# Keys turned by VectorE in 32x32 blocks, and first-softmax scores as 32-row by 32-column array tiles in three banks

## The chip, the cores and the metric

The kernel runs on one core of a Trainium2 chip. The metric is the device time in microseconds of one execution. Three runs of the kernel before took 1696.77, 1696.78 and 1698.92 us; their median is 1696.78 us.

## What is computed

Three stages follow each other, all in fp32: an attention with 32 learned "pack" rows per head, a gated feed-forward layer, and a second feed-forward layer.

```python
# q, k, v: (8 batches, 8 heads, 576, 64); p: (8, 8, 32, 64)
def sm_attn(qq, kk, vv):
    s = scale * np.matmul(qq, kk.transpose(0, 1, 3, 2))
    s = s - np.max(s, axis=-1, keepdims=True)
    a = np.exp(s)
    a = a / (np.sum(a, axis=-1, keepdims=True) + 1e-09)
    return np.matmul(a, vv)
p_packed = sm_attn(p, k, v)                # first softmax: 32 x 576 scores per head
out = sm_attn(q, p_packed, p_packed)       # second softmax: 576 x 32 scores per head
...
x = out as (4608 tokens, 512); xn = x / rms(x) * rms_g
x = (silu(xn @ w_gate) * (xn @ w_val)) @ w_out          # 512 -> 1536 -> 512
h = x @ w_in2; return (max(h,0) + alpha*min(h,0)) @ w_out2   # 512 -> 2048 -> 512
```

The change is in the first softmax alone, up to its exponentials: `p @ k^T`, the row maximum, and exp. The weights and `w_in2`, `w_out2` arrive as 64-bit numbers and are narrowed on the chip.

## The kernel before, in words

**Main loop.** Tokens are worked in 12 chunks `c` (`CH`, L49 to L60) of 512 or 320 columns, three for each two batches. In each chunk a loop over `f` from 0 to 11 (L951) does a gate block `ps_g` (`blk_in`, L967), a value block `ps_v` (L978), and, for the `f` before, the block back to the model width `ps_y` (`blk_out`, L985). Each product is three matmuls of split operands (`mm3`, L121 to L123). VectorE combines gate and value at L975 and L979, ScalarE takes the high part `hh` and VectorE the low part `hl`.

**Work between the blocks.** The attention of later batches is cut into steps of generators ("chains"): `k_steps` for the first softmax of one batch, `q_steps` for the second softmax of a group of tokens. `burst(f)` (L922) emits their TensorE work between the value block and `blk_out`, within a budget of 4 PSUM banks; a weight job `wg_job` takes 2 of them. A step that yields a number waits for a burst with that many left. `work(f, at)` (L875) emits the other steps: `E` (any engine) one per call, `R` (reads of a bank), and `M` and `X` (maximum and exp). In chunks after the first, `M` and `X` come in the call right behind the burst. In chunks 0 and 1 the key chain goes first in a burst, later the query chains do.

**Banks.** Gate, value, weight-job and attention blocks take turns in four PSUM banks (tag `m`, L105), in program order: each new block waits until the last reader of the block four places earlier is done.

**One key chain** (a batch; 8 heads in two groups `g` of 4). `load_p` and `load_kv` bring p and the keys with heads side by side. S1 (L358) and S2 (L367) turn p and the keys with TensorE transposes, 4 and 24 per batch; `evac` copies each bank to SBUF on ScalarE (L116) or VectorE (L118). S3 (L377) makes the scores of two heads at a time with p laid out block-diagonally, so half of the 128 contracted rows meet zeros: 4 matmuls of 288 columns for each group, in two banks. fp32 matmuls appear in the trace as two passes each. MX (L387, L388) takes the maximum on VectorE, EX (L397) the exponentials on ScalarE, RZ (L403, L407) the reciprocal of the sum. S4 (L415) turns the exponentials, S5 (L424) multiplies by v, S6 (L446) prepares the second softmax.

**Prologue.** Before the main loop, the chain of batch 0 and the query chains of the first 512 tokens run alone (L688 to L748), beside the first weight loads. All loads are issued by SP, in program order.

Of the kernel before, what the change touches and what calls it, by code (L numbers as in the profile page):

```python
# [8 lines left out]
F32 = mybir.dt.float32  # L9
# [9 lines left out]
def attention_moe_moe2_kernel(ctx, tc, q, k, v, p, w_gate, w_val, w_out, rms_g, w_in2, w_out2, alpha, out):  # L19
# [105 lines left out]
    with tc.manual_schedule():  # L125
# [6 lines left out]
        pbd = ap.tile([64, H // 2, 128], F32, name="pbd")  # L132
        ppbd = [ap.tile([128, G, HG, D], F32, name=f"ppbd{i}") for i in range(2)]
        ppB = [ap.tile([128, HG, NP], F32, name=f"ppB{i}") for i in range(2)]
        nc.vector.memset(pbd, 0.0)
# [8 lines left out]
        def load_p(b):  # L144
            for e in range(2):
                for g in range(G):
                    nc.sync.dma_start(
                        out=pbd[(e ^ g) * NP:(e ^ g) * NP + NP, 2 * g:2 * g + 2, e * D:(e + 1) * D],
                        in_=p[b].rearrange("(g c e) n d -> e g n c d", g=G, e=2)[e, g],
                    )  # L150
# [4 lines left out]
        def load_kv():  # L155
# [5 lines left out]
            if nm == "k":  # L161
                t = t.rearrange("p (r h) d -> p r h d", r=KR)
                for h in range(HG):
                    nc.sync.dma_start(out=t[:, :, h], in_=src[:, h])
            else:
                t = t.rearrange("p (h r) d -> p h r d", r=KR)
                nc.sync.dma_start(out=t, in_=src)
# [180 lines left out]
        def k_steps(b, bk):  # L348
            par = b % 2
            yield 2  # L350
            pT = ap.tile([128, H // 2, 64], F32, tag="pT", name="pT")
            s1, kT, E1, E1T = {}, {}, {}, {}
            st = [ap.tile([128, 8], F32, tag=f"st{g}", name=f"st{g}") for g in range(G)]

            def S1():
                t = bk()
                for c in range(4):
                    nc.tensor.transpose(t[:, c * 64:(c + 1) * 64], pbd[:, c, :], ident[0:64, 0:64])  # L358
                return lambda: evac(pT, t[:, 0:256].rearrange("p (c x) -> p c x", c=4), True)

            def S2(g, n):
                t = bk()
                if n == 0:
                    kT[g] = ap.tile([128, 2 * S], F32, tag="kT", name="kT")
                for m in range(4):
                    c, r = divmod(4 * n + m, KR)
                    nc.tensor.transpose(  # L367
                        t[:, m * KP:(m + 1) * KP], kv_t[b, "k", g][:, r, 2 * c:2 * c + 2, :], ident[0:KP, 0:KP]
                    )
                return lambda: evac(kT[g][:, n * 384:(n + 1) * 384], t[:, 0:384], n % 2 == 0 or b < 2)  # L370

            def S3(g):
                w = S // 2
                for hf in range(2):
                    t = bk()
                    for c in range(2):
                        nc.tensor.matmul(  # L377
                            out=t[c * 64:(c + 1) * 64, 0:w],
                            lhsT=pT[:, 2 * g + c, :],
                            rhs=kT[g][:, c * S + hf * w:c * S + (hf + 1) * w],  # L380
                            start=True, stop=True,
                        )
                    s1[g, hf] = t

            def MX(g):
                for hf in range(2):
                    nc.vector.tensor_reduce(out=st[g][:, hf:hf + 1], in_=s1[g, hf][:, 0:S // 2], axis=AX.X, op=ALU.max)  # L387
                nc.vector.tensor_scalar(  # L388
                    out=st[g][:, 2:3], in0=st[g][:, 0:1], scalar1=st[g][:, 1:2], scalar2=-scale,
                    op0=ALU.max, op1=ALU.mult,  # L390
                )

            def EX(g):
                w = S // 2
                E1[g] = ap.tile([128, S], F32, tag="E1", name="E1")
                for hf in range(2):
# [87 lines left out]
            if b + 1 < B:  # L484
                load_p(b + 1)
# [237 lines left out]
        for n in range(9):  # L723
            ck.run()
            if n == 7:
                qa.run()
# [505 lines left out]
```

## Time and profile before

| | |
|---|---|
| median of three runs | 1696.78 us |
| the profiled execution | 1693.4 us, span 1691.6 us, mean granted clock 0.98 |
| TensorE matmul busy | 1610.1 us, 95% of the span |
| VectorE, ScalarE, GpSimd busy | 1129.2 us (67%), 708.5 us (42%), 356.0 us (21%) |
| chain that ended last | TensorE 74%, VectorE 13%, ScalarE 4% |
| DMA queue | 52.3% of 16 engines' span |

The profile comes from one execution, 1.8 us of it outside the span. Busy time of TensorE counts the tail of each pipelined matmul, so it overstates the work a little; where one block ends and the next begins is read from the timeline or the chain. The key chains of batches 1 to 7 lie between 46 and about 677 us of the span.

### The profile page before, as it was taken

Reading aid. Unit: us, or ns where it says so; the run is one execution under the profiler, and the core shown is the slowest. Engines: PE = TensorE matmul, PEld = TensorE weight load, DVE = VectorE, ACT = ScalarE, POOL = GpSimd, SP = SyncE. Lnnn points to the kernel's source line nnn. Section 1 sums busy time; section 2 is a strip of 40 time slices with the busy share of each in tenths; the row PEclk is TensorE's granted clock in tenths of the full one; section 3 lists DMA queues with packets and bytes.
Section 4 is the critical chain, followed back from the end, with each engine's and each line's share of the span. In section 5 each row is a group of like instructions: output and inputs, shape, how many; then the busy total and the mean of one; then the engine's idle time right before and its main releaser. Section 6 shows DMA issues by size and latency. Waiting matters only on the chain.

```text
span 1691.6 us, 28163 instructions
## 1 busy us (share of the span) xinstructions
PE 1610.1 (95%) x10378; PEld 1353.6 (80%) x10378; DVE 1129.2 (67%) x2109; ACT 708.5 (42%) x1529; POOL 356.0 (21%) x321
## 2 busy tenths in 40 slices
PE   7787998999999899999998999999999999999999
PEld 5455787888878888888887788888888888997997
DVE  4776456676566665656548787767767775776775
ACT  3564445555455454555444332511242133215224
POOL 1442123332323322334125553000000000000000
PEclk8798899999999999999999999999999999999999
DMA  9975455735555353551211666654373446567553
GB/s 226 284 217 166 132 154 169 194 88 171 160 165 180 76 159 122 162 166 34 95 45 75 220 237 218 222 189 150 137 264 140 168 146 227 198 213 261 187 181 125
DMA packets 224249, 284.46 MB, mean 168 GB/s; under 512 B 94064, under 2 KB 112496, under 8 KB 224112
## 3 DMA queue, kind: packets, MB, share of 16 engines
q1 hardware_dynamic: 224112, 282.66, 52.3%
q8 instruction: 82, 1.34, 0.3%
q14 instruction: 55, 0.45, 0.1%
HBM read 230.17 MB, written 52.43 MB: 167 GB/s over the span
## 4 chain that ended last, share of the span: by engine, by line
PE 74%; DVE 13%; ACT 4%; issue 2%; DMA 2%; POOL 1%; SPq 1%; DVEq 0%; ACTq 0%; POOLq 0%
PE ps_y L121 11%; PE ps_y L122 10%; PE ps_y L123 10%; PE ps_g L122 10%; PE ps_g L123 10%; PE ps_g L121 10%; PE ps_wg L669 2%; PE ps_v L121 2%; PE ps_v L122 2%; PE ps_v L123 2%; DVE s L979 2%; DVE hl L112 1%; ACT hh L109 1%; DVE s L975 1%; DVE yl L112 1%
## 5 line engine op out<-in xcount | busy, mean ns | idle before, releaser
L307 POOL TENSOR_TENSOR in_l<-w_raw,in_h 128x512 fp32r<-128x512 f32 x131 | 172.7, 1318 | 384.3 <-ACT in_h L109 349.5
L121 PE MATMUL ps_y<-hh,in_h 128*128 128x320 f32 (+1 forms) x576 | 208.9, 363 | 5.7 <-ACT hh L109 5.7
L109 ACT ACTIVATE hh<-tl 128x512 fp32r<-128x512 f32 (+1 forms) x80 | 47.1, 588 | 377.7 <-DVE tl L1040 377.7
L122 PE MATMUL ps_y<-hl,in_h 128*128 128x320 f32 (+1 forms) x576 | 198.0, 344 | 0.6
L123 PE MATMUL ps_y<-hh,in_l 128*128 128x320 f32 (+1 forms) x576 | 197.1, 342 | 0.0
L975 DVE SCALAR_TENSOR_TENSOR s<-s,ps_g 128x320 f32<-128x320 f32 (+1 forms) x132 | 71.3, 540 | 155.2 <-ACT s L970 154.9
L109 ACT ACTIVATE hh<-s 128x320 fp32r<-128x320 f32 (+1 forms) x144 | 75.5, 524 | 207.8 <-DVE s L979 207.8
L112 DVE TENSOR_TENSOR hl<-s,hh 128x320 fp32r<-128x320 f32 (+1 forms) x144 | 89.1, 619 | 85.0 <-ACT hh L109 85.0
L121 PEld LDWEIGHTS ps_y<-hh,in_h 128*128 128x128 f32 x576 | 110.9, 193 | 35.5 <-issue 19.5
L121 PE MATMUL ps_g<-yh,w 128*128 128x512 f32 (+1 forms) x336 | 125.3, 373 | 4.4 <-ACT th L1138 4.4
L121 PE MATMUL ps_g<-xh,wgh 128*128 128x256 f32 (+3 forms) x384 | 118.7, 309 | 9.6 <-ACT wgh L109 2.8
L109 ACT ACTIVATE in_h<-w_raw 128x512 fp32r<-128x512 f32 x144 | 90.4, 628 | 87.0 <-PE ps_y L122 83.8
L123 PE MATMUL ps_g<-yh,w 128*128 128x512 f32 (+1 forms) x336 | 124.8, 372 | 0.0
L122 PE MATMUL ps_g<-yl,w 128*128 128x512 f32 (+1 forms) x336 | 124.8, 371 | 0.0
L122 PE MATMUL ps_g<-xl,wgh 128*128 128x256 f32 (+3 forms) x384 | 117.8, 307 | 3.4 <-DVE xl L112 3.3
L122 PEld LDWEIGHTS ps_y<-hl,in_h 128*128 128x128 f32 x576 | 111.3, 193 | 8.9 <-DVE hl L112 2.2
L123 PEld LDWEIGHTS ps_y<-hh,in_l 128*128 128x128 f32 x576 | 110.9, 193 | 8.6
L123 PE MATMUL ps_g<-xh,wgl 128*128 128x256 f32 (+3 forms) x384 | 117.1, 305 | 0.7 <-DVE wgl L112 0.7
L121 PE MATMUL ps_v<-xh,wgh 128*128 128x256 f32 (+3 forms) x384 | 116.1, 302 | 0.0
L122 PE MATMUL ps_v<-xl,wgh 128*128 128x256 f32 (+3 forms) x384 | 115.9, 302 | 0.0
L123 PE MATMUL ps_v<-xh,wgl 128*128 128x256 f32 (+3 forms) x384 | 115.8, 302 | 0.0
L121 PE MATMUL ps_y<-in_h,hh 128*128 128x512 f32 x288 | 112.3, 390 | 1.4 <-ACT in_h L109 1.2
(184 smaller groups left out, 4044.1 us busy)
## 6 DMA issues: line engine op xcount, KB each, us to landing
w<-w_dram SPq DMA_DIRECT2D x224, 256.0 KB, 5.2
gv_raw<-gv_dram SPq DMA_DIRECT2D x168, 256.0 KB, 3.7
o_raw<-w_dram SPq DMA_DIRECT2D x52, 512.0 KB, 4.0
w_dram<-w SPq DMA_DIRECT2D x88, 256.0 KB, 2.2
w<-in_moe_w_out_dram SPq DMA_DIRECT2D x28, 512.0 KB, 4.1
kt<-in_k_dram SPq DMA_DIRECT2D x64, 144.0 KB, 4.0
vt<-in_v_dram SPq DMA_DIRECT2D x16, 576.0 KB, 5.7
qt<-in_q_dram SPq DMA_DIRECT2D x32, 256.0 KB, 5.4
```

The costliest lines, as they stand in the source:

```text
L109: nc.scalar.activation(out=hi, in_=src, func=ACTF.Copy)
L112: nc.vector.tensor_tensor(out=lo, in0=src, in1=hi.bitcast(F32), op=ALU.subtract)
L121: nc.tensor.matmul(out=o, lhsT=lh, rhs=rh, start=first, stop=False, skip_group_check=more)
L122: nc.tensor.matmul(out=o, lhsT=lh, rhs=rl, start=False, stop=False, skip_group_check=more)
L123: nc.tensor.matmul(out=o, lhsT=ll, rhs=rh, start=False, stop=last, skip_group_check=more)
L307: nc.gpsimd.tensor_tensor(out=l, in0=raw[u], in1=h.bitcast(F32), op=ALU.subtract)
L669: nc.tensor.matmul(out=ts[g][h * NP:(h + 1) * NP, :], lhsT=ppG[b][e * D:(e + 1) * D, c_, :], rhs=us[c_][e * D:(e + 1) * D, :], start=True, ...
L975: nc.vector.scalar_tensor_tensor(out=s, in0=s, scalar=1.0, in1=tg, op0=ALU.add, op1=ALU.mult)
L979: nc.vector.tensor_tensor(out=s, in0=s, in1=tv, op=ALU.mult)
```

## The change

S1 and S2 become VectorE transposes in 32x32 blocks, straight from the loaded tile to SBUF: one instruction for p (96 rows, a copy of p's 32 rows in each 32-row group) and one per head for the keys (96 partitions x 384). They are `E` steps and take no bank. A turned block holds, on partitions of row group `a`, 32 of the 64 head dimensions against the 32 keys of that group. S3 then makes, for each group of heads, 2 halves of the head dimension x 4 heads x 3 row groups = 24 matmuls of 32 rows, 32 columns and 192 moving columns; each row group writes a bank of its own, and S3 is emitted as a step of 3 banks. MX and EX work on three banks of 192 columns in place of two of 288. p is loaded three times over, right behind S1; keys of a batch after the first arrive as one transfer for four heads with runs of 1536 bytes; the chain has 7 counted steps in place of 11.

```diff
         def load_p(b):
-            for e in range(2):
-                for g in range(G):
-                    nc.sync.dma_start(out=pbd[...], in_=p[b].rearrange("(g c e) n d -> e g n c d", g=G, e=2)[e, g])
+            for a in range(KP // NP):
+                nc.sync.dma_start(
+                    out=p4[a * NP:(a + 1) * NP].rearrange("n (h d) -> n h d", h=H),
+                    in_=p[b].rearrange("h n d -> n h d"))
...
+            t = t.rearrange("p (h r) d -> p h r d", r=KR)
+            n_h = 1 if nm == "k" and b == 0 else HG
+            for h in range(0, HG, n_h):
+                nc.sync.dma_start(out=t[:, h:h + n_h], in_=src[:, h:h + n_h])
...
             def S1():
+                nc.vector.transpose(pT, p4)
+            def S2(g, h):
+                if h == 0:
+                    kT[g] = ap.tile([KP, HG, KR * D], F32, tag="kT", name="kT")
+                nc.vector.transpose(kT[g][:, h], kv_t[b, "k", g][:, h].rearrange("p r d -> p (r d)"))
             def S3(g):
+                for a in range(NA):                      # NA = 3, W = 192
+                    s1[g, a] = bk()
+                for e in range(2):
+                    for h in range(HG):
+                        for a in range(NA):
+                            rows = slice(a * 32, a * 32 + 32)
+                            o = (g * HG + (h ^ g)) * D + e * 32
+                            nc.tensor.matmul(
+                                out=s1[g, a][h * NP:(h + 1) * NP, 0:W].rearrange("p (r x) -> p r x", r=KR),
+                                lhsT=pT[rows, o:o + 32],
+                                rhs=kT[g][rows, h ^ g].rearrange("p (r d) -> p r d", r=KR)[:, :, e * 32:e * 32 + 32],
+                                start=e == 0, stop=e == 1, tile_position=(a * 32, h * NP))
             def MX(g):
+                for a in range(NA):
+                    nc.vector.tensor_reduce(out=st[g][:, a:a + 1], in_=s1[g, a][:, 0:W], axis=AX.X, op=ALU.max)
+                # then two tensor_scalar in place of one
             def EX(g):
+                for a in range(NA):                      # three Exp of 192 in place of two of 288
...
-            yield from two(S1, lambda: S2(0, 0))
-            yield 2
-            yield from two(lambda: S2(0, 1), lambda: S2(0, 2))
+            S1()
+            if b + 1 < B:
+                load_p(b + 1)
+            for h in range(HG):
+                yield E
+                S2(0, h)
             load_kv()
-            yield 2
+            yield 3
             S3(0); yield M; MX(0); yield X; EX(0)
-            yield 2
-            yield from two(lambda: S2(1, 0), lambda: S2(1, 1))
+            for h in range(HG):
+                yield E
+                S2(1, h)
+            load_kv()
             RZ(0)
             yield 2
-            yield from two(lambda: S2(1, 2), lambda: S4(0, 0))
+            yield from two(lambda: S4(0, 0), lambda: S4(0, 1))
...
-                    if ch.done >= 7 and q_open.get(ch.b - 2) or ch.done == 10 and ...
+                    if ch.done >= 3 and q_open.get(ch.b - 2) or ch.done == 6 and ...
```

Three places in the instruction order follow. On TensorE, at `f` = 6 of chunk 3 (361 us in the trace of before), between the value block and the block back, before:

```order
L121 MATMUL ps_v<-xh,wgh 128x320
L122 MATMUL ps_v<-xl,wgh 128x320
L123 MATMUL ps_v<-xh,wgl 128x320
L628 MATMUL ps_at<-ident,s_3713 128x128 x2
L377 MATMUL ps_at<-kT,pT 64x288 x4
L121 MATMUL ps_y_3715<-hh,in_h 128x320
```

and now, with L622 for L628 and the new S3 as L367:

```order
L121 MATMUL ps_v<-xh,wgh 128x320
L122 MATMUL ps_v<-xl,wgh 128x320
L123 MATMUL ps_v<-xh,wgl 128x320
L622 MATMUL ps_at<-ident,s_3720 128x128 x2
L367 MATMUL ps_at<-kT,pT 32x192 x24
L121 MATMUL ps_y_3722<-hh,in_h 128x320
```

The score block stands at the same place, with 24 small matmuls for 4; the banks taken between two gate blocks are now value, 1 and 3, where they were value, 1 and 2. On VectorE at the same `f`, before (L975 and L979 combine gate and value, L387 is MX, L632 reads the bank of L628):

```order
L975 SCALAR_TENSOR_TENSOR s<-s,ps_g 128x320
L979 TENSOR_TENSOR s<-s,ps_v 128x320
L112 TENSOR_TENSOR hl<-s,hh 128x320
L387 TENSOR_REDUCE st_3653<-ps_at 128x1 x2
L388 TENSOR_SCALAR st_3653<-st_3653 128x1
L632 TENSOR_TENSOR A2T<-A2T,ps_at 128x512
```

and now (L969, L973, L377, L626 for the same four):

```order
L969 SCALAR_TENSOR_TENSOR s<-s,ps_g 128x320
L973 TENSOR_TENSOR s<-s,ps_v 128x320
L112 TENSOR_TENSOR hl<-s,hh 128x320
L377 TENSOR_REDUCE st_3794<-ps_at 128x1 x3
L378 TENSOR_SCALAR st_3794<-st_3794 128x1
L381 TENSOR_SCALAR st_3794<-st_3794 128x1
L626 TENSOR_TENSOR A2T<-A2T,ps_at 128x512
```

The reader of the other chain's bank stands behind five instructions of MX in place of three. On SP, the first loads, before (`pbd` is p, `w` the 64-bit weights):

```order
L147 DMA pbd<-in_p_dram 32x2x64 x4
L164 DMA kt<-in_k_dram 96x6x64 x8
L167 DMA vt<-in_v_dram 96x4x384
L714 DMA g_col<-in_moe_rms_g_dram 128x4x1
L167 DMA vt<-in_v_dram 96x4x384
L178 DMA qt<-in_q_dram 128x8x64 x2
L205 DMA w_177<-in_moe_w_gate_dram 128x512
```

and now:

```order
L145 DMA p_93<-in_p_dram 32x8x64 x3
L162 DMA kt<-in_k_dram 96x384 x8
L162 DMA vt<-in_v_dram 96x4x384
L708 DMA g_col<-in_moe_rms_g_dram 128x4x1
L145 DMA p_93<-in_p_dram 32x8x64 x3
L162 DMA vt<-in_v_dram 96x4x384
L162 DMA kt<-in_k_dram 96x4x384
L173 DMA qt<-in_q_dram 128x8x64 x2
L200 DMA w_205<-in_moe_w_gate_dram 128x512
```

p and half of the keys of batch 1 now stand ahead of the first queries and weights; they wait for the buffers that S1 and S2 of batch 0 read.

## Rows read from the trace of the kernel before

**Rows 1.** Windows by stage: us, then busy us (and instructions) by engine, clock, DMA.

```profile
0.00:46.00 46.00, 31.25 (x298) 22.71 (x306) 21.59 (x56) 18.64 (x51) 8.80 (x15) 0.83 0.95 216
46.00:180.00 134.00, 110.27 (x665) 75.59 (x650) 93.35 (x167) 74.48 (x146) 46.50 (x34) 0.87 0.68 216
180.00:700.00 520.00, 499.66 (x4395) 427.12 (x4394) 323.17 (x706) 265.62 (x620) 156.92 (x127) 0.99 0.52 150
```

**Rows 2.** Groups of TensorE, 180 to 700 us: busy us, mean ns, then idle before.

```profile
L669 PE MATMUL ps_wg<-gv_raw,ppG 64*32 64x512 f32 x480 | 34.3, 601 | 0.0
...
L367 PE MATMUL ps_at<-ident,kt 96*128 96x96 f32 x133 | 15.8, 253 | 2.0 <-DVE s L975 1.7
L377 PE MATMUL ps_at<-kT,pT 128*64 128x288 f32 x96 | 14.7, 418 | 0.0
```

**Rows 3.** The same 520 us in one window, for line L358 (S1) alone: PE, PEld.

```profile
180.00:700.00 520.00, 2.29 (x20) 1.61 (x20) 0.99 0.52 150
```

**Rows 4.** Pieces of the chain that ended last: start us, us, what.

```profile
361.48 1.12 PE ps_at L377 x8
...
366.54 0.81 PE ps_at L424 x48
...
421.28 0.81 PE ps_at L367 x8
...
672.32 1.02 PE ps_wg L669 x16
```

**Rows 5.** Groups of VectorE and ScalarE, whole span: busy us, mean ns, then idle before.

```profile
L975 DVE SCALAR_TENSOR_TENSOR s<-s,ps_g 128x320 f32<-128x320 f32 x96 | 46.5, 484 | 88.7 <-ACT s L970 88.5
...
L116 ACT ACTIVATE kT<-ps_at 128x384 f32<-128x384 f32 x31 | 15.0, 485 | 1.0 <-PE ps_at L367 1.0
...
L397 ACT ACTIVATE E<-ps_at,st 128x288 f32<-128x288 f32 x29 | 14.3, 497 | 25.5 <-DVE st L388 20.3 <-PE ps_y L367 2.3 <-DVE A L566 2.3
...
L387 DVE TENSOR_REDUCE st<-ps_at 128x1 f32<-128x288 f32 x29 | 11.9, 449 | 9.9 <-PE ps_at L377 9.8
...
L581 DVE STREAM_TRANSPOSE A2T<-A 128x512 f32<-128x512 f32 x16 | 11.3, 703 | 0.1
...
L118 DVE COPY kT<-ps_at 128x384 f32<-128x384 f32 x12 | 6.6, 550 | 0.0
```

**Rows 6.** Timeline around the score block of chunk 3, f = 6: start us, us, instruction.

```profile
360.89 0.49 DVE L975 SCALAR_TENSOR_TENSOR s<-s,ps_g 128x320 f32<-128x320 f32 x1 [1.33 <-ACT s L970]
...
361.41 1.19 PE L377 MATMUL ps_at<-kT,pT 128*64 128x288 f32 x8
361.48 0.49 DVE L979 TENSOR_TENSOR s<-s,ps_v 128x320 f32<-128x320 f32 x1
...
362.53 0.41 PE L121 MATMUL ps_y<-hh,in_h 128*128 128x320 f32 x1
...
362.91 0.82 DVE L387 TENSOR_REDUCE st<-ps_at 128x1 f32<-128x288 f32 x2
...
363.77 0.21 DVE L388 TENSOR_SCALAR st<-st 128x1 f32<-128x1 f32 x1
...
363.90 0.68 DVE L632 TENSOR_TENSOR A2T<-A2T,ps_at 128x512 f32<-128x512 f32 x1
...
364.40 0.31 PE L121 MATMUL ps_g<-xh,wgh 128*128 128x320 f32 x1
```

**Rows 7.** Waits of TensorE up to 700 us: total us, times, longest us.

```profile
PE ps_g L121 <- ACT E L397: 2.1, 3, 1.5
```

**Rows 8.** Pieces of the chain that ended last, in the first chunk.

```profile
84.05 1.28 ACT L346
...
102.82 0.62 SPq L164
...
105.50 5.06 DMA w<-in_moe_w_val_dram
```

**Rows 9.** Timeline of SP in the prologue: start us, us, instruction.

```profile
10.44 3.28 SPq L178 DMA_DIRECT2D qt<-in_q_dram  x2
```

More of the change, by code (lines that the diff above doesn't have):

```diff
@@ L349, in k_steps @@
             par = b % 2
-            yield 2
-            pT = ap.tile([128, H // 2, 64], F32, tag="pT", name="pT")
+            yield E
+            pT = ap.tile([KP, H * D], F32, tag="pT", name="pT")
             s1, kT, E1, E1T = {}, {}, {}, {}
             st = [ap.tile([128, 8], F32, tag=f"st{g}", name=f"st{g}") for g in range(G)]
+            NA, W = KP // 32, KR * 32
             def S1():
[L356 to L370, printed above, removed]
@@ L372, in S3 @@
-            def S3(g):
[L373 to L383, printed above, removed]
+                nc.vector.transpose(pT, p4)
@@ L385, in MX @@
             def MX(g):
-                for hf in range(2):
-                    nc.vector.tensor_reduce(out=st[g][:, hf:hf + 1], in_=s1[g, hf][:, 0:S // 2], axis=AX.X, op=ALU.max)
+                for a in range(NA):
+                    nc.vector.tensor_reduce(out=st[g][:, a:a + 1], in_=s1[g, a][:, 0:W], axis=AX.X, op=ALU.max)
                 nc.vector.tensor_scalar(
-                    out=st[g][:, 2:3], in0=st[g][:, 0:1], scalar1=st[g][:, 1:2], scalar2=-scale,
+                    out=st[g][:, 0:1], in0=st[g][:, 0:1], scalar1=st[g][:, 1:2], scalar2=None, op0=ALU.max
+                )
@@ L390, in MX @@
+                nc.vector.tensor_scalar(
+                    out=st[g][:, 3:4], in0=st[g][:, 0:1], scalar1=st[g][:, 2:3], scalar2=-scale,
                     op0=ALU.max, op1=ALU.mult,
@@ L393, in EX @@
             def EX(g):
-                w = S // 2
                 E1[g] = ap.tile([128, S], F32, tag="E1", name="E1")
-                for hf in range(2):
+                for a in range(NA):
                     nc.scalar.activation(
-                        out=E1[g][:, hf * w:(hf + 1) * w], in_=s1.pop((g, hf))[:, 0:w], func=ACTF.Exp,
-                        bias=st[g][:, 2:3], scale=scale, accum_out=st[g][:, 3 + hf:4 + hf],
+                        out=E1[g].rearrange("p (r a x) -> p r a x", r=KR, a=NA)[:, :, a],
+                        in_=s1.pop((g, a))[:, 0:W].rearrange("p (r x) -> p r x", r=KR), func=ACTF.Exp,
+                        bias=st[g][:, 3:4], scale=scale, accum_out=st[g][:, 4 + a:5 + a],
                     )
@@ L722, in attention_moe_moe2_kernel @@
         loads_to(8)
-        for n in range(9):
+        for n in range(6):
             ck.run()
-            if n == 7:
+            if n == 4:
                 qa.run()
@@ L912, in k_turn @@
                 for ch in [ch for ch in chains["k"] if ch.kind is not None][:1]:
-                    if ch.done >= 7 and q_open.get(ch.b - 2) or ch.done == 10 and n_job[0] < NJ * (ch.b - 1):
+                    if ch.done >= 3 and q_open.get(ch.b - 2) or ch.done == 6 and n_job[0] < NJ * (ch.b - 1):
                         pass
```

39 lines of the change are left out of this document (14 added, 25 removed).

## The prediction

> **What bounds the kernel now.** I read the stages first. From 180 to 700 us, where six of the eight key chains run (batches 2 to 7), TensorE is busy 499.7 of 520 us at a clock of 0.99, VectorE 323 and ScalarE 266 [rows 1]. There a microsecond taken from TensorE comes off the time, unless a wait takes its place. Before that, from 46 to 180 us, it is another matter: TensorE is busy 110 of 134 us at a mean clock of 0.87, VectorE 93, and the chain of waits passes through weight conversions, loads and ScalarE [rows 1, 8]. In the first 46 us no engine is busy more than 31 us and the DMA share is 0.95 [rows 1]. So the change has to be priced in three stretches, with three prices.
>
> Next, the groups of TensorE for the steps that go, then the chain for the time from one block to the next (busy time counts each tail, which overlaps the next block), and last the timeline around one score block, to see which bank is read when.
>
> **TensorE, batches 2 to 7.** In the chain eight key transposes take 0.81 us [rows 4]; a batch has 24, so 2.43 us. A score block takes 1.12 us for its eight passes [rows 4]; two per batch are 2.24 us. S1 was busy 2.29 us for 20 transposes, five batches, 0.46 us each [rows 3]; eight key transposes are busy 8 x 15.8 / 133 = 0.95 us [rows 2] where the chain has 0.81, so I count S1 at 0.39 us. Together 5.06 us a batch, 30.4 us for six. (Busy times alone would make 2.85 + 2.45 + 0.46 = 5.76 us, 34.6 us for six [rows 2, 3].)
>
> What comes is 12 score blocks of 24 matmuls, 48 passes of 192 columns each, on twelve array tiles. No row shows such tiles. S5 has 48 passes of 64 columns on four tiles in 0.81 us, 17 ns a pass; a weight job has 16 passes of 512 columns on eight tiles (two row groups by four column groups) in 1.02 us [rows 4]. Scaled by columns the weight job gives 1.02 x 9216 / 8192 = 1.15 us at eight tiles and 0.77 us at twelve. If the three row groups took turns, S5's pace at three times the columns would give 2.43 us. The bounds are 0.77 and 2.43 us; the weight job, which does run two row groups side by side, is nearer in form, and S5's pace of passes will not be beaten by much, so I take 1.0 us. Twelve blocks: 12.0 us. TensorE gives back 30.4 - 12.0 = 18.4 us.
>
> The Trainium skill (TensorEngine Tiling (Array Packing), Instruction Overhead) states about 60 cycles of overhead for each matmul, however short. An estimate from that at 2.4 GHz is 48 x 25 ns = 1.2 us a block, and the sum would lose 2.4 us; S5's 17 ns a pass lies below that figure, so I stay with the rows.
>
> **VectorE and ScalarE, batches 2 to 7.** A transpose of 128x512 takes 703 ns [rows 5]. One of 96x384 lies between three quarters of that, 0.53 us, and the whole of it; I take 0.56, near the lower end, as 449 ns for 288 columns against 484 for 320 show time going with columns [rows 5]. Eight are 4.5 us, p's 0.70. Three maxima of 192 in place of two of 288: 3 x 0.345 - 2 x 0.449 = 0.14 us (0.30 to 0.45 each), and two more small instructions of 0.21 us for each group [rows 6], 1.1 us a batch in all. Two copies of 0.55 us go [rows 5]. Net 5.2 us a batch, 31 us for six: VectorE goes from 323 to 354 us in that stretch, 68 to 70%. I cost this at nothing: a transposed head is issued one per call between the blocks, and VectorE sits idle 88.7 us before 96 instructions of L975, 0.92 us each, waiting for ScalarE [rows 5]. If that cover is gone, each piece is late by up to 0.56 us. ScalarE loses four copies of 0.485 us and gains two shorter Exp of about 0.4 us a batch [rows 5]; nothing waits on that difference.
>
> **What is late next: banks.** A score block now holds three of the four banks that gate and value blocks share. In seven of the twelve blocks the order puts another step's bank ahead of it, so its third bank is the one of the value block just done. Its reader, L979, runs from 361.48 to 361.97, while the score block began at 361.41 [rows 6]; since the three row groups are interleaved, the block waits some 0.55 us at its third matmul. Its end is then 361.41 + 0.55 + 1.0 = 362.96, and `blk_out` ends 1.87 us later (362.53 to 364.40), at 364.83. The next gate block wants the bank of the other step. Where that step is the one of L628 (four blocks), MX starts at 362.96 and takes three starts of 0.31 (0.41 for 288 columns, less the columns) and two of 0.13 (L388 to L632); L632's 0.68 us then ends at 364.83 [rows 6], 0.15 us late at most. Where it is the query transposes (three blocks), their copy stands on ScalarE behind three Exp: 364.2 + 3 x 0.40 + 0.5 = 365.9, 1.1 us late. So 4 x 0.7 + 3 x 1.65 = 7.8 us. In chunk 1 (two blocks) the key chain goes first; its third bank is the gate's, free when L975 ends at 361.38, and the next gate block takes the first score bank: 0.4 us each. Three blocks stand alone, 0.25 us each. Sum 9.3 us. What goes: the waits for Exp, 2.1 us [rows 7], and those before key transposes, 2.0 us [rows 2]. Net 5.2 us more waiting.
>
> Emptying is already long beside filling: 0.82 us of maxima, then two Exp, for a block of 1.12 us [rows 4, 6]. The Trainium skill (TensorEngine Tiling (Array Packing), PSUM Bottleneck) says that tiling speeds up TensorE but not the emptying of its banks, which may then become the bottleneck. The trace agrees so far, and the last rival below is where that would end.
>
> **First chunk and prologue.** Four key loads, each some 0.62 us as the one shown, stand in the chain just ahead of a weight load that it waits for [rows 8]; one is left of them, -1.9 us. The order has two ScalarE table loads fewer (one query step meets the key step in one switch to Exp); one of 1.28 us is on the chain [rows 8], -1.3 us. VectorE gets 6.3 us more for batch 1, where no copy of its own goes, in a stretch where it is busy 93 of 134 us; I let a fifth of it count, +1.3. In the prologue the query loads, issued at 10.44 us [rows 9], stand behind transposes that wait for the first maximum, some 3 us later; with DMA near full until then the data come about 0 to 2 us late, but 1536-byte runs for the keys make the same bytes cheaper afterwards. I take 0. Sum -2 us, bounds -8 and +8.
>
> **Sum.** -18.4 + 5.2 - 2 = -15.2 us. The profiled execution took 1693.4 us (span 1691.6 and 1.8 around it), which makes 1678.2; the median of the runs lies 3.4 us above it, so 1681.6 us for the median. Score blocks of 0.81 to 1.15 us move it by -2.3 to +1.8, the waits by some 3.5 and the first stretch by 5 either way: 1674 to 1689 for this case.
>
> **Rivals.**
>
> *More than that.* The new waits stay away (VectorE reaches the maxima earlier, since S2's copies are gone) and the first chunk gains 7 us: -18.4 - 4.1 - 7 = -29.5, 1667 us. For it: ScalarE and SP both lose work. Against: the three-bank order is fixed.
>
> *The first stretch loses.* Queries come 3 us late, and VectorE's 6.3 us lands on the conversions whole: +8 there, 1691.6 us. For it: DMA 0.95, VectorE 70% busy [rows 1]. Against: a shorter SP queue later.
>
> *Row groups take turns*, so the tiles don't do what the change says: 12 x 2.43 = 29.2 us, -1.2 + 5.2 - 2 = +2, 1699 us. Against: weight jobs on two row groups, whose 16 passes of 601 ns [rows 2] fit into 1.02 us only if about nine run side by side, more than the four column groups of one row group.
>
> *Slower: the three banks are emptied too late.* At every score block the third bank (0.55 us), the copy behind three Exp (1.1) and a VectorE queue that holds a turned head and a query piece ahead of the maxima (0.56 + 0.70) add up to 2.9 us: 12 x 2.9 - 4.1 = 30.8, less 20.4, makes +10.4, 1707 us. It decides from 24.5 / 12 = 2.0 us a block. For it: a `blk_out` of 1.87 us is the only cover. Against: of 12 such blocks before, only three made a gate block wait for Exp, 1.5 us at most [rows 7].
>
> **How the numbers follow.** Forecast 0.54, more 0.17, first stretch 0.10, row groups 0.08, banks 0.11. A measurement tells 0.2%, 3.4 us, from no change. Faster: 0.54 + 0.17 + half of 0.10 = 0.76. Within 0.2%: 0.05 + 0.08 = 0.13. Slower: 0.11. The range 1665 to 1697 leaves out a third of the second case, the fifth and half of the fourth, about 0.2.
>
> **What would show it.** Right: no TensorE transposes of keys; score blocks of 0.8 to 1.2 us from first pass to the next block; TensorE waits for Exp, the query copy or the value block's reader of 5 to 13 us in sum from 180 to 700 us; the stretch from 180 us to the last key chain shorter by about 13 us; later stages unchanged. Wrong: score blocks near 2.4 us; waits of 2 us at most of them; a first gate block 3 us or more later than before, or turned heads that make the reader of a gate or value block late.

## The result, and the profile after

The changed kernel takes 1706.13 us (median of four runs, 1705.54 to 1709.33) where the kernel before takes 1696.78: a ratio of 1.006, 95% interval 1.0041 to 1.0078. It is slower, by 9 us; the forecast was 15 us faster, and the time lies outside its range. The profiled span went from 1691.6 to 1703.5 us.

The stages of the changed kernel, in the columns of [rows 1]:

```profile
0.00:46.00 46.00, 31.44 (x340) 22.79 (x340) 25.58 (x67) 14.47 (x40) 8.10 (x14) 0.74 0.95 223
46.00:180.00 134.00, 101.72 (x670) 68.97 (x671) 95.64 (x184) 68.12 (x141) 47.61 (x35) 0.84 0.66 210
180.00:700.00 520.00, 491.53 (x4665) 416.31 (x4664) 342.07 (x774) 252.86 (x608) 153.67 (x124) 0.98 0.51 147
```

From 180 to 700 us TensorE has become less busy (491.5 for 499.7 us) and VectorE busier (342 for 323). If TensorE had been given back time, the stretch would have become shorter with TensorE as dense as before. It is idle more instead.

To see where, I compare the starts of VectorE's value product (L979 before, L973 after) at the same places of the program. The difference to before, in us, worked out from the timelines of one profile of each kernel:

| kernel | first f | chunk 1 | chunk 2 | chunk 4 | chunk 6 | chunk 8, f = 7 |
|---|---|---|---|---|---|---|
| changed | +4.5 | +5.3 | +3.2 | +10.9 | +10.2 | +11.5 |
| loads in order, table early | -1.7 | -0.5 | +0.1 | +8.3 | +8.0 | +8.5 |
| keys turned once | +4.7 | +2.6 | -2.1 | +0.3 | -3.2 | -4.3 |
| before, with GpSimd's help | +1.6 | +1.4 | +1.8 | +0.8 | +0.4 | -3.9 |
| all helps, keys turned once | +0.7 | -1.2 | -6.6 | -6.2 | -9.6 | -13.6 |

The first row: 4.5 us are lost in the prologue, under one in the first chunk, some 6 in the loop, almost nothing behind it. The other rows are experiments, below. In what follows, T1, T2 and T4 are steps of a query chain on TensorE: the query transposes (L528), the query scores (L545, two banks) and the products behind the softmax (L586, two banks); xl (L112) is the low part of a chunk's input x.

The groups that answer to [rows 2, 5], whole span, busy us, mean ns, idle before:

```profile
L357 DVE STREAM_TRANSPOSE kT<-kt 96x384 f32<-96x384 f32 x64 | 35.1, 558 | 0.3 <-DMA kt<-in_k_dram 0.3
L377 DVE TENSOR_REDUCE st<-ps_at 128x1 f32<-128x192 f32 x42 | 12.3, 348 | 0.2
L389 ACT ACTIVATE E<-ps_at,st 128x192 f32<-128x192 f32 x42 | 17.2, 418 | 24.6 <-DVE st L381 24.6
L969 DVE SCALAR_TENSOR_TENSOR s<-s,ps_g 128x320 f32<-128x320 f32 x96 | 46.3, 482 | 74.8 <-ACT s L964 74.3
```

The durations that I estimated are right: 0.558 us for a turned head (taken: 0.56), 0.348 for a maximum (0.345). The idle time ahead of the gate product, which I had named as the cover, fell only from 88.7 to 74.8 us over the 96 instructions [rows 5]. So it was there, and most of it still is, and the work beside it cost time all the same. The turned heads themselves waited only 0.3 us in all for their loads.

The waits of TensorE from 180 to 700 us (us in total, times, longest):

```profile
PE ps_at L367 <- DVE A L556: 8.1, 3, 5.2
PE ps_g L122 <- DVE xl L112: 6.9, 7, 1.3
PE ps_at L367 <- DVE s L969: 3.2, 4, 1.1
PE ps_v L121 <- DVE ppG L452: 2.8, 2, 1.4
...
PE ps_g L121 <- ACT E L389: 0.5, 2, 0.3
```

The large ones all end with VectorE. The wait for Exp of [rows 7], 2.1 us before, is down to 0.5 us. The wait for `ppG` (a value block stands still until VectorE has read the bank of S6) is 2.8 us in two places and does not occur in the kernel before.

One place of the first and third kind, chunk 3, f = 3. First the chain that ends at 360 us, its pieces in order (start, us, what):

```profile
345.55 0.49 DVE kT L357
346.04 0.58 DVE A L560
...
347.31 0.70 DVE s L566
...
348.03 1.16 DVE s L567
...
349.21 0.25 DVE s L568
349.46 0.63 DVE A L556 x2
350.09 0.58 DVE A L570
350.67 0.59 DVE s L558
351.26 0.41 DVE s L969
```

and TensorE's timeline there:

```profile
347.97 0.31 PE L123 MATMUL ps_v<-xh,wgl 128*128 128x320 f32 x1
349.82 0.83 PE L367 MATMUL ps_at<-kT,pT 32*32 32x192 f32 x4 [1.54 <-DVE A L556]
351.71 1.11 PE L367 MATMUL ps_at<-kT,pT 32*32 32x192 f32 x44 [1.05 <-DVE s L969]
352.75 0.53 PE L121 MATMUL ps_y<-hh,in_h 128*128 128x320 f32 x1
```

The score block wants three banks. Two of them hold the query scores of the f before, which L556 reads; that stands on VectorE behind four steps of the other query chain and a turned head. The third is the gate's, and its reader L969 stands behind two more query steps. The block takes 2.93 us and `blk_out` starts 4.8 us after the start of the value block's last matmul. Not all of this is the turned head's: the step at L567 took 1.16 us where the same step later took 0.17, beside a GpSimd step (last section), so some 1.0 us of the first stop is GpSimd's; the same happened at the other block of this kind (chunk 6, 566.88 us, 1.14 us). With the keys turned once, below, the first stop here is still 1.03 us, 0.5 less.

Then TensorE's clock falls: windows of the changed kernel, and after them one of the kernel before, of the same chunk, an f later (columns as above):

```profile
350.00:354.00 4.00, 2.94 (x53) 2.04 (x52) 3.36 (x8) 0.47 (x1) 0.00 (x0) 0.86 0.03 8
354.00:358.00 4.00, 4.00 (x21) 3.81 (x19) 3.90 (x12) 2.79 (x9) 0.65 (x1) 0.71 0.00 0
```

```profile
350.00:354.00 4.00, 2.74 (x22) 2.36 (x20) 3.36 (x6) 1.93 (x8) 2.92 (x2) 1.00 0.22 72
```

Behind the two stops the granted clock was 0.71 in a window in which TensorE was busy throughout: `blk_out` took 3.3 us where it took 1.9 before, at the lower of the two levels (1.2 GHz) for most of it. Before, TensorE idled 1.3 us of one window and the clock stayed at 1.00. Four such dips from 184 to 720 us (at 199, 353, 401 and 571 us) cost 8.5 us of full clock in the changed kernel, two before (194 and 566 us) 5.1.

Of the twelve score blocks of the loop, one is clean and takes 1.08 us to the next block's start (as one of the first chunk does); six take 1.55 to 1.75, one 2.0, the three that stand alone 2.3, 2.9 and 3.1 (the longer two behind a T2 of the f before), and the first one 8.7. That last one is in part older than the change: VectorE stood still for a late weight load, and TensorE behind it. The last of the lines below is from the kernel before, where a T2 stood at this place and TensorE waited 3.7 us.

```profile
199.32 0.43 DVE L218 TENSOR_SCALAR w<-w 128x512 int32<-128x512 int32 x1 [7.64 <-DMA w<-in_moe_w_in_dram]
...
200.16 0.84 PE L367 MATMUL ps_at<-kT,pT 32*32 32x192 f32 x2 [5.23 <-DVE A L556]
...
195.05 1.67 PE L551 MATMUL ps_at<-qT,ppB 64*32 64x256 f32 x16 [3.67 <-DVE s L975]
```

### The profile page after: what moved, and what is told of

It reads as the page before. It is cut to its first block, busy times and chain, and to the rows that moved or that the text cites. A ratio compares the mean times of both kernels' runs of the same rounds, so it can differ in the third digit from the quotient of the medians.

```text
span 1703.5 us, 29018 instructions
## 1 busy us (share of the span) xinstructions
PE 1604.5 (94%) x10794; PEld 1343.6 (79%) x10794; DVE 1161.7 (68%) x2216; ACT 693.1 (41%) x1513; POOL 357.6 (21%) x321
## 4 chain that ended last, share of the span: by engine, by line
PE 69%; DVE 16%; ACT 5%; DMA 3%; issue 2%; POOL 1%; SPq 0%; DVEq 0%; ACTq 0%; POOLq 0%
PE ps_y L121 10%; PE ps_y L122 10%; PE ps_y L123 10%; PE ps_g L122 9%; PE ps_g L123 9%; PE ps_g L121 9%; PE ps_wg L663 2%; DVE s L973 2%; PE ps_v L121 2%; PE ps_v L122 2%; PE ps_v L123 2%; DVE hl L112 2%; ACT hh L109 2%; DVE s L969 1%; DVE kT L357 1%
## 5 line engine op out<-in xcount | busy, mean ns | idle before, releaser
L969 DVE SCALAR_TENSOR_TENSOR s<-s,ps_g 128x320 f32<-128x320 f32 (+1 forms) x132 | 71.0, 538 | 140.8 <-ACT s L964 140.3
L112 DVE TENSOR_TENSOR hl<-s,hh 128x320 fp32r<-128x320 f32 (+1 forms) x144 | 86.9, 603 | 85.0 <-ACT hh L109 85.0
L122 PE MATMUL ps_y<-in_l,hh 128*128 128x512 f32 x288 | 113.1, 393 | 1.4 <-DMA in_l<-os_dram 0.8
```

What stands on the lines that cost most here:

```text
L112: nc.vector.tensor_tensor(out=lo, in0=src, in1=hi.bitcast(F32), op=ALU.subtract)
L122: nc.tensor.matmul(out=o, lhsT=lh, rhs=rl, start=False, stop=False, skip_group_check=more)
L969: nc.vector.scalar_tensor_tensor(out=s, in0=s, scalar=1.0, in1=tg, op0=ALU.add, op1=ALU.mult)
```

## Experiments

Each run was timed against the kernel before on its own chip; the ratio and its interval are to that. The theories: **A**, the prologue's loss is the load order, and **A'**, the Exp table; **B**, the loop's loss is the three banks; **C**, it is VectorE's time.

**The prologue.** Batch 1's p and first key load go behind the queries (first), the Exp table is loaded early (second), and both (third).

```diff
-            if b + 1 < B:
+            if 0 < b < B - 1:
                 load_p(b + 1)
...
                 S2(1, h)
-            load_kv()
+            if b:
+                load_kv()
             RZ(0)
             yield 2
+            if b == 0:
+                load_p(1)
+                load_kv()
```

```diff
         tick[0] = const.tile([128, 1], F32, name="tick")
+        preload(ACTF.Exp)
```

> The changed kernel, with batch 1's p and its first key load issued in the prologue after the first Exp and its turned keys, so behind the queries and the first weights, as in the kernel before. Theory A (of the 4.5 us that the first gate-block mark is late after the change, the load order is the cause: query loads issued 2.4 us later, query transposes 4.1 us later): the wait of TensorE for query tiles ends about 4 us earlier, the first weight job comes at 45.5 to 46.5 us in place of 49.6, and the time falls by 3 to 5 us, to about 1702. Rival A' (the Exp table load that now stands on ScalarE's path, and the idle 2.9 us of TensorE with the half clock behind it): no more than 1 us gained, first weight job at 48.5 us or later.

> The changed kernel with one Exp of a single column put ahead of the first key chain, so that the Exp table is loaded before the first score block is ready. Rival A' expects S4's wait for Exp (2.94 us) to shrink by 1.3 us or more, the clock to stay at 1.00 until about 26 us, and the first weight job 2 to 4 us earlier than 49.6 us. Theory A (load order) expects the wait for Exp to shrink but the first weight job to move by less than 1 us, since it waits for query loads; time within 1 us of the changed kernel.

> The changed kernel with both of the edits that moved little by themselves: batch 1's p and first key load behind the queries and first weights, and the Exp table loaded early. Theory A+A' (each hides the other: with the loads in order the first chain is bound by the table load and TensorE's half clock behind it, with the table early it is bound by the queries' loads): the first gate-block mark, 60.9 us in the changed kernel, 60.0 and 61.5 us with one edit alone, comes at 57.5 us or earlier, and the time falls by 2.5 to 5 us, to 1701 to 1703.5. Rival (something else, as the threefold load of p or VectorE's queue, holds the prologue): mark at 59.5 us or later, time within 1.5 us of the changed kernel.

Measured: 1707.33 us (1.006, 1.0039 to 1.0080) with the loads in order, 1705.85 (1.0059, 1.0039 to 1.0078) with the table early, both no different from the changed kernel; 1702.88 (1.004, 1.0028 to 1.0052) with both. A line of the kernel before, then lines of the changed kernel on ScalarE, TensorE and SP, then of the kernel with both edits:

```profile
0.73 1.28 ACT L116 ACT_TABLE_LOAD   x1 [0.73 <-PEq L1216]
```

```profile
9.77 1.28 ACT L389 ACT_TABLE_LOAD   x1 [9.77 <-DVE st L381]
...
12.44 1.52 PE L411 MATMUL ps_at<-ident,E 128*96 128x128 f32 x6 [2.94 <-ACT E L389]
...
31.39 0.66 PE L528 MATMUL ps_y<-ident,qt 128*128 128x128 f32 x4 [2.97 <-DMA qt<-in_q_dram]
...
11.94 2.21 SPq L173 DMA_DIRECT2D qt<-in_q_dram  x2
```

```profile
0.73 1.28 ACT L341 ACT_TABLE_LOAD   x1 [0.73 <-PEq L1215]
...
11.22 0.86 PE L411 MATMUL ps_at<-ident,E 128*96 128x128 f32 x6 [1.66 <-ACT E L389]
...
26.26 2.19 PE L532 MATMUL ps_y<-ident,qt 128*128 128x128 f32 x8 [3.02 <-DMA qt<-in_q_dram]
...
7.97 4.04 SPq L173 DMA_DIRECT2D qt<-in_q_dram  x2
```

Two chains run side by side, the queries' loads and the first key chain, and each hid the other: with one mended, the first mark moved by -0.9 and +0.7 us, with both by -6.1. The copies that the change removed had loaded the table at 0.73 us; without them it waits for the first score block, and TensorE, idle 2.9 us, runs the next steps at the lower level of the clock (six transposes 1.52 for 0.86 us). In the whole time about 3 us are left of it; the intervals of 1.004 and 1.006 overlap, so the size is less sure than the mark. A and A' were each half right.

**Keys turned once.** For batches 1 to 7 the turned heads are left out; steps and banks stay.

```diff
             def S2(g, h):
+                if b:
+                    kT[g] = kT0[1]
+                    return
```

> The changed kernel with keys turned for batch 0 only: batches 1 to 7 take batch 0's second group of turned keys for both groups (so their scores are those of other keys), and the 56 transposes of 0.57 us are left out of VectorE's queue; steps, banks, matmuls, maxima and Exp stay where they are. Theory C: TensorE's waits for the low part of x (6.9 us), for the reader L556 inside score blocks (8.1 us) and for L969 fall by half or more, the loop from the first chunk's second gate block to the end of the key chains takes 8 to 14 us less, and the time falls below 1699 us. Theory B: the three banks are still waited for, waits inside score blocks stay above 12 us, and the time falls by less than 4 us.

Measured: 1690.17 us, 0.9958 (0.9942 to 0.9974): 16 us less than the changed kernel for 56 x 0.558 = 31 us of VectorE. Its last stretch and two of its waits:

```profile
180.00:700.00 520.00, 498.70 (x4769) 423.73 (x4768) 328.41 (x742) 260.00 (x620) 157.95 (x127) 0.99 0.53 154
```

```profile
PE ps_at L372 <- DVE A L561: 7.0, 3, 4.9
PE ps_g L122 <- DVE xl L112: 4.0, 6, 1.1
```

C's time came. Its way did not: the waits for L556 (now L561) and for x's low part, which I had expected to halve, fell by 4 us of 15. The 13 us of the loop (table of marks) are spread over the start-to-start times of all blocks: score blocks 1.5, gate blocks 2.3, value 1.8, out 2.1, T4 2.3, weight jobs 1.7, S4 0.7. Part of that is the clock, whose dips cost 5.1 us in place of 8.5; the rest is in many places of which none is large. The wait for `ppG` stays at 2.8 us.

**Two banks**, with the keys turned as in the change, and turned once. The third key group goes through row group 1 again, behind the other two, into the second bank.

```diff
-                for a in range(NA):
-                    s1[g, a] = bk()
-                for e in range(2):
+                s1[g, 0], s1[g, 1] = bk(), bk()
+                s1[g, 2] = s1[g, 1][:, W:2 * W]
+                for e, as_ in ((0, (0, 1)), (1, (0, 1)), (0, (2,)), (1, (2,))):
...
+                            ra = min(a, 1)
...
-            yield 3
+            yield 2
             S3(0)
```

> The changed kernel with score blocks in two banks: the third key group's matmuls go through row group 1 again (with row group 1's keys, so these scores are not the right ones) into columns 192 to 383 of the second bank, behind the second group's. Maxima, Exp and turned heads stay as many and as large. The step asks for two of four bank places in place of three. The block itself gets longer, from 1.08 us to between 1.3 and 1.6 us, 4 to 8 us in all. Theory B (loss by three banks whose readers on VectorE are late: of 17 us of waiting inside score blocks 11.3 us are for readers on VectorE): waiting inside score blocks falls below 6 us, and the time falls by 3 to 8 us in spite of the longer blocks. Theory C (VectorE's queue, long by the turned heads, makes all its readers late wherever they stand): the waits move to other blocks, the time rises by 2 to 8 us.

> The changed kernel with both the score blocks in two banks (third key group through row group 1 again) and the keys turned for batch 0 only, so neither the scores nor their keys are the right ones. It stands against the run with keys turned once, 1690.2 us. Theory B2 (the third bank costs some 10 us of waiting inside the blocks even where VectorE is not short): waits inside score blocks fall from 9.7 to 4 us or less and the time falls to 1682 to 1688 us, though each block is up to 0.5 us longer. Rival (the third bank is cheap, the one long wait there is behind a late load): 1689 us or more.

Measured: 1710.75 us (1.0078, 1.0055 to 1.0102) and 1693.48 (0.9987, 0.9977 to 0.9998). The score blocks did become short: 1.46 to 1.49 us at eight of twelve places, 21.2 us in all for 30.0. The time did not. TensorE's waits in the first of the two kernels, 180 to 700 us, and one window of it:

```profile
PE ps_g L122 <- DVE xl L112: 8.0, 7, 2.0
PE ps_at L421 <- DVE s L970: 5.1, 2, 2.8
PE ps_at L412 <- DVE A L557: 4.7, 1, 4.7
PE ps_g L121 <- ACT E L390: 4.1, 3, 2.2
```

```profile
204.00:234.00 30.00, 28.51 (x218) 24.29 (x219) 13.80 (x35) 9.33 (x25) 5.10 (x4) 0.54 0.42 110
```

The same readers are waited for, now by other steps. (In this profile a wait of 4.7 us was followed by 28 us at half clock, with TensorE busy 28.5 of 30 us; other executions need not have it: the six runs lie between 1704.9 and 1715.4 us.) With VectorE relieved, no wait of more than 0.2 us is left inside the twelve score blocks, where 9.5 us were, and the time is no better either: 1693.5 against 1690.2. So B does not explain the time, and B2's 1682 to 1688 us did not come. But the third bank isn't shown to be free. From chunk 2 to the last mark of the table the profiles with two banks are 4.9 and 2.6 us ahead of their partners with three; they lose more than that in chunk 1 (14 and 5 us), where the late weight load and the slow clock lie. And the wait for `ppG` is in neither of them. A few us of the third bank may thus be hidden behind chunk 1; no run here keeps the two apart.

**VectorE's time added to the kernel before**, as 56 turned heads that nothing reads, and only their calls.

```diff
+            def turn(g):
+                for h in range(HG if b else 0):
+                    yield E
+                    s_ = ap.tile([KP, W], F32, tag="kx", name="kx")
+                    nc.vector.transpose(s_, kv_t[b, "k", g].rearrange("p r h d -> p (r h d)")[:, h * W:(h + 1) * W])
...
+            yield from turn(0)
             yield from two(S1, lambda: S2(0, 0))
```

> The kernel before with the changed kernel's turned heads added: 56 VectorE transposes of 96x384, 0.57 us each, into a tile that nothing reads, one per call between blocks, ahead of S1 and behind the first Exp of batches 1 to 7; keys still go through TensorE. Theory C (VectorE's time between the blocks is not free): slower than before by 6 to 14 us, with more TensorE waits for the low part of x and for VectorE's bank readers. Theory B (three banks per score block are the cause, VectorE's time is covered): within 3 us of before.

> The kernel before with the calls of the added turned heads, but without the transposes: the key chain is as late as with them, VectorE has nothing more to do. Theory C (VectorE's time costs): within 8 us of before, so that most of the 29 us of the run with the transposes is VectorE's 32 us. Rival C4 (the later key chain costs, not VectorE): slower than before by 15 us or more.

Measured: 1724.74 us (1.0173, 1.0160 to 1.0186) and, calls alone, 1713.44 (1.0102, 1.0088 to 1.0116). So 17 of the 29 us come from the later key chain, which C had not expected and C4 had, and the other 11 to 12 from VectorE's 31 us, some 0.37 a microsecond. Of what the calls cost, 10.7 us are lost by the first mark of chunk 1, half of them at the end of chunk 0, where the chain of batch 1 is run out at once, and the rest in chunks 6 to 8. The run with the calls alone, and the same two places of the kernel before:

```profile
174.14 2.08 PE L598 MATMUL ps_at<-ppbd,A2T 64*128 64x128 f32 x16 [6.27 <-DVE A2T L587]
...
179.38 0.69 PE L634 MATMUL ps_at<-ident,s 128*128 128x128 f32 x2 [3.16 <-POOL s L629]
```

```profile
162.67 2.08 PE L592 MATMUL ps_at<-ppbd,A2T 64*128 64x128 f32 x16 [5.62 <-DVE A2T L581]
...
167.88 0.69 PE L628 MATMUL ps_at<-ident,s 128*128 128x128 f32 x2 [3.13 <-POOL s L623]
```

The two long waits are in both kernels, nearly as long; what the calls do is put them 11.5 us later, behind the rest of the key chain.

**Other places for the same VectorE work.** Turned heads only where no query step is due; then, with the helps below, two to a call; then none in a chunk's last f.

```diff
+                        elif ch in chains["k"] and ch.kind == E and (
+                            f == NF - 1 or any(o.kind in (E, X) for o in chains["q"])
+                        ):
+                            break
```

```diff
             for h in range(HG):
-                yield E
+                if h % 2 == 0:
+                    yield E
                 S2(0, h)
```

```diff
+                        elif ch in chains["k"] and ch.kind == E and (
+                            c > 0 and f == NF - 1
+                        ):
+                            break
```

> The changed kernel in which a turned head is issued only in calls where no query chain has a VectorE or Exp step due, and none at the last f of a chunk. VectorE's work stays the same, only its bunching goes; score blocks come some f later. Theory C1 (pile-ups: two or three pieces in one call make the readers late): TensorE's waits for x's low part fall from 6.9 to 4 us or less, waits inside score blocks fall by 3 us or more, the time falls by 3 to 8 us. Rival C2 (the sum of VectorE's work counts, wherever it is put, or the new places of the score blocks are as bad): within 2 us of the changed kernel.

> As the run with all three helps (1693.8 us), with two turned heads in each call, so four calls per batch in place of eight; VectorE's work stays the same, score blocks and what follows come one to three f earlier. Theory C4 (late key chains cost): 1684 to 1690 us. Theory C1 (bunched pieces cost): 1696 us or more. If only VectorE's sum counts: within 2 us of 1693.8.

> As the run with all three helps, and no turned head in the calls of a chunk's last f, behind the first chunk (VectorE's work stays the same; score blocks stay at their places but for the last chain, which ends three f later). If turned heads ahead of x's low part make it late: TensorE's waits for it fall from 6.9 to 3 us or less, and the time by 2 to 5 us against that run. If other pieces stand ahead of it there: waits of 5 us or more, time within 1.5 us of that run.

Measured: 1712.09 us (1.010, 1.0085 to 1.0115), 1701.47 (1.003, 1.0019 to 1.0041) and 1692.40 (0.9979, 0.9967 to 0.9991). The first missed C1: from chunk 1 to the middle of chunk 6 it ran 11 us faster than before, but its chains ended later: 5.6 us went in the first chunk, 5.4 in the second half of chunk 6, and more behind chunk 7, where the last chain ran out. The second came out at C1's number by something else: a query copy on ScalarE stood behind the late weight load, and TensorE waited 8.5 us for it.

```profile
204.85 0.43 DVE L218 TENSOR_SCALAR w<-w 128x512 int32<-128x512 int32 x1 [9.82 <-DMA w<-in_moe_w_in_dram]
...
206.91 0.88 PE L411 MATMUL ps_at<-ident,E 128*96 128x128 f32 x3 [8.48 <-ACT qT L536]
```

These two runs moved every step, so they tell little about bunching, and neither C1 nor C4 is settled by them. The third moved only the last chain; waits for x's low part fell from 6.9 to 4.3 us (3 or less expected), the time by 1.4, which its interval does not tell from none.

**VectorE's work given to GpSimd**: the subtraction and the product of the query softmax behind the first chunk, in the changed kernel, with the prologue's edits too, and in the kernel before.

```diff
-            nc.vector.tensor_tensor(
+            eng = nc.gpsimd if steady[0] else nc.vector
+            eng.tensor_tensor(
                 out=av, in0=av, in1=mx.unsqueeze(2).to_broadcast([128, G * nb, NP]), op=ALU.subtract
```

> The changed kernel with two steps of the query softmax, the subtraction of the maximum and the product with the reciprocal (0.65 to 0.69 us each on VectorE, some 30 of them behind the first chunk, about as much as two thirds of the turned heads), given to GpSimd, which is busy a quarter of that stretch. Theory C: the time falls by 4 to 10 us. Rival C3 (GpSimd holds VectorE up: in the changed kernel a VectorE step of 0.17 us took 1.15 us and ended with a GpSimd subtraction of 1.27 us): VectorE's steps get longer or the query chains later, the time rises or stays within 2 us.

> The changed kernel with the three edits that helped: load order and early Exp table (together -3.3 us) and two softmax steps on GpSimd (-10.6 us). If the two causes are apart, the prologue's chain and VectorE's queue, the gains add: 1706.1 - 3.3 - 10.6 = 1692 us, 1690 to 1695, and the kernel is faster than the one before. Rival (both act on the same waits of the first chunk): 1695 us or more.

> The kernel before with the same two softmax steps on GpSimd: some 20 us less for VectorE, no turned heads. Theory C as a price per microsecond of VectorE (some 0.5): faster than before by 5 to 11 us. Rival C5 (VectorE's time only costs beyond some load, which the kernel before does not reach): within 3 us of before.

Measured: 1695.54 us (1.0002, 0.9993 to 1.0010), 1693.82 (0.9987, 0.9978 to 0.9996) and 1687.98 (0.9958, 0.9944 to 0.9972). Some 20 us of VectorE (26 steps of about 0.7 us, 14 small ones) are worth 10 us in the changed kernel and 8 in the one before, though GpSimd takes longer (the kernel before with the help):

```profile
L578 POOL TENSOR_TENSOR A<-A,s 128x512 f32<-128x512 f32 x13 | 14.4, 1108 | 0.0
```

C3 and C5 fall: VectorE's time had a price already in the kernel before. That kernel with this help is the fastest here that leaves nothing out, 0.42% below the one before. The helps of prologue and GpSimd together came to 1693.8 us, where adding makes 1692 and 1690 to 1695 was expected. Not all of the gain in the changed kernel is plain VectorE time: the steps held up by GpSimd (1.16 for 0.17 us) no longer meet it, and the two score blocks behind a T2 fall from 2.9 and 3.1 us to 1.7 and 1.5.

**What the change would be worth without its price**: all three helps, keys turned once.

> The run with all three helps, and the keys turned for batch 0 only (the scores of the other batches are those of other keys): what the change would be worth if turning cost VectorE nothing behind batch 0. If the causes add: 1693.8 - 16 + some of the help by GpSimd, which is then needed less: 1678 to 1684 us, near the forecast of 1681.6. If TensorE's gain is not there: above 1688 us, no better than the kernel before with the help by GpSimd alone (1688.0).

Measured: 1677.90 us, 0.9891 (0.9877 to 0.9904).

```profile
180.00:700.00 520.00, 502.06 (x4819) 425.00 (x4818) 320.38 (x725) 263.39 (x631) 186.13 (x160) 0.99 0.53 154
```

Here TensorE is busier than it was before [rows 1], and gets further in the same 520 us (13.6 us at the last mark of the table). But this run has GpSimd's help too, so its partner is the kernel before with that help, 1688.0 us: with turning at no cost to VectorE and the prologue mended, the change is worth 10 us, where the forecast had 15. Most of the gain that the forecast counted is there, and VectorE's time ate it in the changed kernel; some 5 us are missing even here.

## Why the prediction was wrong

**The step that failed** is "I cost this at nothing": VectorE's net 31 us for six batches, laid beside the idle time ahead of L975. Leaving out the turned heads of seven batches (31 us) gives 16 us back, adding them to the kernel before costs 11 to 12, taking 20 us away gives 8 to 10: 0.35 to 0.5 us for each microsecond, in both kernels. (By VectorE's busy time on the pages of the profiles, where ends that overlap count once, the four differences are 27.8, 24.0, 17.5 and 14.7 us, and the price is 0.5 to 0.6.) For batch 1 the prediction itself let a fifth count; for the other six nothing. The idle time was an average over 96 places [rows 5]. VectorE's steps run in the order of the program, and at a place like chunk 3, f = 3 above, six query steps (one of them held up by GpSimd), a turned head and the readers of three banks stand in one row, and there is none. That one place is an example: by the start-to-start times the price is spread over all blocks. "If that cover is gone, each piece is late by up to 0.56 us" names the price, some half of 56 x 0.56 us; no case of mine carried it by itself.

**The prologue, "I take 0"**: the first mark is 4.5 us late, and 3 us of the time come back with the edits. I had priced the loads and dropped the table: I counted two table loads fewer in the first chunk, and did not see that the early one (0.73 us before, 9.77 us now) moved onto the path. With only the loads in my sum, the hiding of one chain by the other could not show.

**TensorE's 18.4 us** hold. Clean score blocks take 1.08 us (taken: 1.0, bounds 0.77 and 2.43), and the key transposes' 19.0 us from chunk 1 on are gone. That the row groups run side by side is likely, but not shown by 1.08 against 2.43 alone: with three times the columns a pass went from 17 ns in S5 to 22.5 ns here, so S5's pace was no measure of groups that take turns. It is borne out by the two-bank runs, where the third group's passes stand behind the others' and the same 48 take 1.46 us. In the time, the last run shows 10 us against its partner.

**The bank waits, 9.3 us**: at six blocks the third bank alone makes 1.55 to 1.75 us of a block, as worked out (0.55 and 1.0); no gate block waited for the copy behind three Exp (0.5 us of waiting for Exp). Three blocks stand alone, as I had counted, but at 0.25 us each; they take 2.3, 2.9 and 3.1 us, together 5.1 us above the clean 1.08. Twelve blocks take 30.0 us where 12.0 + 9.3 were worked out, 7.6 of the excess over 1.08 behind the late load, which before fell on a T2 and cost 3.7. The wait for `ppG`, 2.8 us, was in no term.

**The rival of the three banks** had the time, 1707 us, by luck, and not the cause: its 2.9 us or more came at three of twelve blocks, one of them the late load's, and two banks did not make the time shorter. Its VectorE queue "that holds a turned head and a query piece" is the part that was right, and it works without the third bank.

The sum with the measured terms: 1681.6 + 16 + 3 = 1701 us. (The 16 include the 1.3 us that the forecast had for batch 1.) Some 5 to 6 us are left, about as much as the last run lacks to the forecast. The nearest are the wait for `ppG` (2.8 us, in the changed kernel and in the last run, not in the kernel before) and the blocks that stand alone with the clock behind them; no run takes either out by itself, and two banks, which remove both, lose as much in chunk 1. So this stays open.

## What to carry to other kernels

Idle time of an engine whose steps run in the order of the program covers added work only where it lies: look at the places where several chains put their pieces in one row, not at the share. When the engine that sets the time waits for the same helper in many small ways, give some of the helper's work away first (8 us here for two steps) and only then move work to it. Of two chains side by side, mend both before you judge either.

## What was not expected of the hardware

A VectorE step on 128x16 took 1.15 us, from 348.03 us on, while GpSimd subtracted, and 0.17 us eight microseconds later without:

```profile
347.88 1.27 POOL L302 TENSOR_TENSOR in_l<-w_raw,in_h 128x512 fp32r<-128x512 f32 x1 [3.92 <-ACT in_h L109]
```

```profile
348.03 1.15 DVE L567 TENSOR_SCALAR s<-s 128x16 f32<-128x16 f32 x1
...
356.26 0.17 DVE L567 TENSOR_SCALAR s<-s 128x16 f32<-128x16 f32 x1
```

It ended at 349.18 us, 0.03 us after GpSimd. Of the 24 times that this step ran in the trace, three met a GpSimd step, and all three took 1.14 to 1.17 us and ended 0.03 us after it. The Trainium skill (Perfetto Trace Analysis, Optimizing Scalar/DVE Operations) says that GpSimd and VectorE share a read port, that a VectorE step which uses two ports holds it as an exclusive lock, and that moving work between the two might therefore not help. These rows agree with such a lock, with the roles the other way round: here GpSimd began first and VectorE waited. The runs with GpSimd's help differ on the advice, by 8 and 10 us.

Twelve 32x32 tiles with three row groups in three banks did 48 passes of 192 columns in 1.08 us, eight tiles in two banks, then four, in 1.46.
